# A second expert for 21 tokens: 128 places in a full array against 32 places in four column tiles

## The chip, the cores and the metric

The kernel runs on one core of one Trainium2 chip. The metric is device time in microseconds (us). A core has TensorE (PE in the profile; its weight loads are listed apart as PEld), VectorE (DVE), ScalarE (ACT), GpSimd (POOL) and SyncE (SP). DMAs are issued from the queues of SP, ACT and POOL and are carried out by 16 DMA engines that all of them share.

## The reference

Attention with one shared key and value head, and then a mixture of experts with two levels of routing:

```python
scores = scale * q @ k.T ; attn = softmax(scores) ; x = (attn @ v)  as [3072, 1024]
g = argmax(x @ w_group)                 # one of 4 groups
e = argmax(x @ w_expert[g])             # one of 4 experts of that group
h = relu(x[tokens of (g, e)] @ w1[g, e])
out[tokens of (g, e)] = group_weight * expert_weight * (h @ w2[g, e])
```

There are 8 batches of 384 tokens, 16 heads of 64, a model width of 1024, and 16 experts with a hidden width of 1024. Because attention averages over its batch, nearly all tokens of a batch choose the same expert. The routing is data dependent, and the inputs are fixed by a seed: evaluated on them, the reference sends all 384 tokens of each of the first seven batches to one expert, and of the last batch 363 tokens to one expert and 21 to a second one.

## The kernel before

**Tiling.** Tokens lie in batches of three blocks (`ST = 3`) of 128. The main loop over half units (line 794) does attention for one batch while the expert of the batch before it runs in the gaps of TensorE. `main_expert` (line 531) takes the most chosen expert of a batch and computes it for all 384 tokens: in its first part (line 479) a 128x128 block of `w1` is the loaded operand and 384 tokens stream by, in its second part (line 493) 128 hidden values by 128 tokens are loaded and 512 columns of `w2` stream by. Tokens that chose another expert get a factor of zero. The result `y` of 128 tokens is written by `store` as four DMAs on SP's queue (line 536), which together are three times four for a batch.

**The last batch.** After the loop (from line 827) there is no attention left for TensorE to share. The order is written out by hand: `advance(n)` runs the next pieces of the main expert, and pieces of the second expert's preparation stand between them. `few_ready` (line 540) builds constants on POOL. `few_turn` (584) turns the batch's activations into token order. `few_flags` and `few_places` (595, 609) find which tokens chose the second expert, number them 0, 1, 2, ... and build for each block of 128 tokens a 0/1 matrix `sel16`, whose column p marks the token on place p; there are 128 places. If more tokens chose it than there are places, `fits` is 0 and the pair is left to the loop at the end. `few_gather` (636) multiplies the token-ordered activations by `sel16`: 24 matmuls of 128 columns (line 643) give `xg`, the chosen tokens' activations with the model width on the partitions; three small matmuls (line 654) give each place its factor `gate` and its row number `at`, which for an empty place lies past the last row. `few_expert` (664) comes after the main expert's end and after `keep_xb(b)` (line 470: the batch's activations, 768 KB, to a scratch tensor in DRAM, on SP's queue). It is in the same form as the main expert, on 128 places: 64 matmuls (line 674) with blocks of `w1` loaded and 128 places streaming, relu by ACT and DVE (lines 680, 682), then 24 matmuls (line 689) with 128 hidden values by 128 places loaded and 512 or 256 columns of `w2` streaming, scaling by DVE and ACT (lines 695, 693), and one indirect DMA on POOL's queue (line 696) that writes each place's row of 4 KB to its row number and skips those past the end.

**Weights.** `load_w` (451) issues two DMAs of POOL's queue for each of `w1` and `w2`, each for half of the contracted blocks (`o` = 0 to 3 and 4 to 7), converting from float32 to bfloat16 on the way. For the second expert they are issued by `load_second(0)` and `load_second(1)` (lines 837, 844), long before `few_expert`. The matmuls that read blocks 4 to 7 wait for the second DMA only.

**The end.** Each engine then reads the number of remaining pairs (line 910) and enters a loop over them (line 911), which for these inputs has no passes.

Of the kernel before, what the change touches and what calls it, by code (L numbers as in the profile page):

```python
# [9 lines left out]
FP32 = mybir.dt.float32  # L10
# [9 lines left out]
def kernel(  # L20
# [23 lines left out]
    NP = B * GE  # L44
    NR = 4096
    assert NR > N
    assert NP == P
# [45 lines left out]
    def xbank():  # L93
        x = ps_x.tile([P, 512], FP32, tag="x", name="x")
        return x
# [354 lines left out]

    def load_w(e, n):
        w = wpool.tile([P, KO, F], BF16, tag=f"w{n + 1}", name="w")
        for o in range(0, KO, 4):
            nc.gpsimd.dma_start(  # L454
                out=w[:, o:o + 4, :], in_=(w1f, w2f)[n][ds(e, 1), :, o:o + 4, :].rearrange("o p c f -> (o p) c f")
            )
        return w
# [73 lines left out]
    def main_expert(b, on_act):  # L531
        w1, w2 = st.pop(("w", b))

        def store(j, y):
            for n in range(QN):
                nc.sync.dma_start(out=out_v[b, j, n], in_=y[32 * n:32 * (n + 1), :])

        yield from expert(st["xb", b], w1, w2, scaled(lambda: st["gsel", b][0], store), any_bank, on_act)

    def few_ready():  # L540
# [4 lines left out]
        for name, t, widths in (  # L545
            ("16", c16, (("eye", P), ("tri", P), ("sel", ST * P), ("f", 4), ("cum", 4), ("parts", 5 * ST))),
            ("32", c32, (
                ("cols", P), ("tri", P), ("sel", ST * P), ("prod", ST * GE), ("ohs", GE), ("rows", ST), ("rest", ST), ("row", 1), ("pos", 4),
                ("f", ST), ("fits", 1), ("gate", 1), ("low", 1), ("at", 1),
            )),  # L550
        ):
# [4 lines left out]
        nc.gpsimd.iota(  # L556
            fw["cols32"], pattern=[[1, P]], base=0, channel_multiplier=0, allow_small_or_imprecise_dtypes=True
        )
# [20 lines left out]
        fw["xt"] = [ppool.tile([P, Dm], BF16, tag="pr", name="xtok") for _ in range(ST)]  # L579
        fw["xg"] = ppool.tile([P, KO, P], BF16, tag="pr", name="xg")  # L580

# [27 lines left out]
    def few_places():  # L609
# [11 lines left out]
        for j in range(ST):  # L621
            nc.vector.tensor_scalar(
                out=fw["sel32"][:, ts(j, P)], in0=fw["cols32"], scalar1=pos[:, j:j + 1], scalar2=fw["f32"][:, j:j + 1],
                op0=ALU.is_equal, op1=ALU.mult,
            )
        nc.scalar.copy(out=fw["sel16"], in_=fw["sel32"])

# [8 lines left out]
    def few_gather():  # L636
        fw = st["few"]
        parts = fw["parts16"].rearrange("p (j t) -> p j t", t=5)
        for half in range(2):
            bank = xbank()  # L640
            for k in range(4):
                for j in range(ST):
                    nc.tensor.matmul(  # L643
                        out=bank[:, ts(k, P)], lhsT=fw["xt"][j][:, ts(4 * half + k, P)], rhs=fw["sel16"][:, ts(j, P)],
                        start=(j == 0), stop=(j == ST - 1),
                    )
            xg = fw["xg"][:, 4 * half:4 * half + 4, :].rearrange("p k t -> p (k t)")
            if half:
                nc.vector.tensor_copy(out=xg, in_=bank[:])
            else:  # L650
                nc.scalar.copy(out=xg, in_=bank[:])
        bank = xbank()
        for j in range(ST):
# [5 lines left out]
        nc.vector.tensor_scalar(  # L659
            out=fw["at32"].bitcast(I32), in0=fw["row32"], scalar1=fw["fits32"], scalar2=float(NR), op0=ALU.mult,  # L660
            op1=ALU.add,
        )

    def few_expert():

        fw = st["few"]
        w1, w2 = st.pop("w_second")
        xg, gate, at_ = fw["xg"], fw["gate32"], fw["at32"].bitcast(I32)
        h_t = pool.tile([P, FO, S], BF16, tag="hT", name="few_h", bufs=1)
        for k0, k1 in ((0, 4), (4, 6), (6, FO)):  # L670
            bank = xbank()[:, 0:(k1 - k0) * P]
            for k in range(k0, k1):
                for ko in range(KO):
                    nc.tensor.matmul(  # L674
                        out=bank[:, ts(k - k0, P)], lhsT=w1[:, ko, ts(k, P)], rhs=xg[:, ko, :],
                        start=(ko == 0), stop=(ko == KO - 1),
                    )
            h, hp = h_t[:, k0:k1, 0:P], bank.rearrange("p (k t) -> p k t", t=P)
            if k0 == 4:
                nc.vector.tensor_scalar(out=h, in0=hp, scalar1=0.0, scalar2=None, op0=ALU.max)  # L680
            else:
                nc.scalar.activation(out=h, in_=hp, func=ACTF.Relu)
        cols = ((0, 512), (512, 768), (768, Dm))
        ys = [xbank()[:, 0:z - a] for a, z in cols]
        y = pool.tile([P, Dm], FP32, tag="y", name="few_y", bufs=3)
        for part in range(2):
            for (a, z), yp in zip(cols, ys):
                for fo in range(4 * part, 4 * part + 4):
                    nc.tensor.matmul(  # L689
                        out=yp, lhsT=h_t[:, fo, 0:P], rhs=w2[:, fo, a:z], start=(fo == 0), stop=(fo == FO - 1)  # L690
                    )
                if part and a:
                    nc.scalar.activation(out=y[:, a:z], in_=yp, func=ACTF.Copy, scale=gate)
                elif part:
                    nc.vector.tensor_scalar(out=y[:, a:z], in0=yp, scalar1=gate, scalar2=None, op0=ALU.mult)
        nc.gpsimd.indirect_dma_start(
            out=out, out_offset=bass.IndirectOffsetOnAxis(ap=at_, axis=0), in_=y[:], in_offset=None,
            bounds_check=N - 1, oob_is_err=False,
        )
# [262 lines left out]
```

## Time and profile before

| | us |
|---|---|
| median of 3 runs | 509.74 |
| the 3 runs | 508.01, 509.74, 509.88 |
| the profiled execution's own time | 508.39 |
| span of the profiled execution (first to last instruction) | 507.0 |

| engine | busy us | share of the span |
|---|---|---|
| PE | 481.5 | 95% |
| DVE | 413.0 | 81% |
| ACT | 321.8 | 63% |
| POOL | 289.6 | 57% |

The chain of waits is the list of what ended last, followed back from the end: 90% of it is PE. A line of the timeline gives the start, the length, the engine, the source line, the operation, `out<-in`, shapes as partitions x elements, a count, and in brackets the idle time before it with what ended it; pieces of one group that lie close together are merged into one line. "128*32" behind a matmul's tensors is the part of the TensorE array that it uses, rows by columns. In a view by windows each row is a stretch of the span with the busy time of each engine, the granted TensorE clock, the busy share of the DMA engines (it can read a little over 1) and the GB/s moved. A DMA's time to landing runs from its issue to its completion. For groups of matmuls the busy time is the union of overlapping executions, so busy time over count is the pitch, and "mean ns of one" is the time from the start of one to its modelled end.

### The profile page before, as it was taken

The page shows a single profiled execution, that of the slowest core. Times are in us where ns is not written, and L with a number is a line of the kernel's source. Part 1 is how long each engine was busy: PE and PEld are TensorE (multiplying, and loading weights), DVE is VectorE, ACT ScalarE, POOL GpSimd, SP SyncE. Part 2 cuts the span into 40 slices and gives each one's busy share as a digit, 9 for nine tenths or more (in the row PEclk, how much of TensorE's full clock was granted, in tenths as well). Part 3 has the DMA queues.
Part 4 walks back from the last instruction along what each step waited for, and adds up shares of the span by engine and source line. Part 5 has one row for each costly group of instructions (what it writes and reads, how often), then busy time and mean ns, then how long its engine had stood idle before and what let it go on. Part 6 is the DMA issues. An engine that isn't in the chain of part 4 may idle for free.

```text
span 507.0 us, 20054 instructions
## 1 busy us (share of the span) xinstructions
PE 481.5 (95%) x8256; PEld 262.1 (52%) x8273; DVE 413.0 (81%) x737; ACT 321.8 (63%) x1002; POOL 289.6 (57%) x524
## 2 busy tenths in 40 slices
PE   7597789999999999999999999999999999999994
PEld 3143356555456455555465455555455455555653
DVE  3889979988899879988899879998799888890630
ACT  4776766677676766676676776676775775753421
POOL 1665955684576664584576654584476654584300
PEclk9999999999999999999999999999999999999998
DMA  7612997399947998389946998389956993089993
GB/s 106 145 26 45 174 239 193 76 160 233 255 86 129 220 237 218 75 157 232 261 84 123 217 243 223 75 143 230 245 116 111 210 241 110 1 155 241 231 243 121
DMA packets 64524, 84.04 MB, mean 166 GB/s; under 512 B 20379, under 2 KB 39963, under 8 KB 64432
## 3 DMA queue, kind: packets, MB, share of 16 engines
q0 software_dynamic: 19152, 37.84, 41.3%
q1 hardware_dynamic: 44320, 44.61, 35.2%
q8 instruction: 66, 1.08, 0.9%
q10 hardware_dynamic: 960, 0.30, 0.3%
q14 instruction: 26, 0.21, 0.1%
HBM read 101.52 MB, written 19.40 MB: 239 GB/s over the span
## 4 chain that ended last, share of the span: by engine, by line
PE 90%; DVE 5%; ACT 3%; issue 1%; POOL 0%; POOLq 0%; ACTq 0%; DVEq 0%
PE x L257 26%; PE s L206 25%; PE x L479 15%; PE x L493 13%; PE sb L493 4%; PE x L280 3%; ACT pr L220 3%; DVE nmx L217 2%; PE sb L479 2%; DVE ring L241 2%; PE x L674 1%; PE x L100 1%; PE x L689 1%; PE x L145 0%; PE x L643 0%
## 5 line engine op out<-in xcount | busy, mean ns | idle before, releaser
L235 POOL TENSOR_SCALAR pr<-pr,rinv 128x384 f32<-128x384 f32 x384 | 218.3, 588 | 146.0 <-DVE rinv L231 133.2
L220 ACT ACTIVATE pr<-s,nmx 128x384 f32<-128x384 f32 x384 | 218.0, 579 | 131.5 <-DVE nmx L217 120.0
L217 DVE TENSOR_REDUCE nmx<-s 128x2 f32<-128x768 f32 x192 | 174.3, 948 | 45.7 <-PE s L206 44.6
L241 DVE STREAM_TRANSPOSE ring<-pr 128x768 f32<-128x768 f32 x192 | 175.4, 952 | 0.1
L206 PE MATMUL s<-kt,qt 64*64 64x384 f32 x1536 | 148.9, 496 | 13.3 <-ACT pr L220 12.3
L257 PE MATMUL x<-ring,v_sb 32*64 32x256 f32 x4608 | 137.7, 378 | 0.2
L257 PEld LDWEIGHTS x<-ring,v_sb 32*64 32x64 f32 x4608 | 101.6, 131 | 43.0 <-issue 23.2
L206 PEld LDWEIGHTS s<-kt,qt 64*64 64x64 f32 x1536 | 48.5, 132 | 82.6 <-ACT pr L220 44.4
L220 ACT ACTIVATION_READ_ACCUMULATOR pr<-s,nmx 128x1 f32 x384 | 77.9, 203 | 0.0
L479 PE MATMUL x<-xb,w 128*128 128x384 bf16 x448 | 76.6, 326 | 0.0
L479 PEld LDWEIGHTS <-w 128*128 128x128 bf16 x512 | 47.7, 98 | 42.2 <-issue 12.6
L493 PE MATMUL x<-w,h_t 128*128 128x512 bf16 x276 | 64.7, 380 | 0.6
L493 PEld LDWEIGHTS <-h_t 128*128 128x128 bf16 x384 | 35.7, 98 | 52.0 <-issue 11.9
L454 POOL DMA_DIRECT2D w<-in_moe_w_dram x36 | 27.9, 784 | 10.8 <-issue 9.0
L271 ACT COPY xt<-x 128x256 f32<-128x256 f32 x96 | 28.9, 385 | 2.8 <-PE x L257 2.7
L485 ACT ACTIVATE h_t<-x 128x384 bf16<-128x384 f32 x56 | 25.4, 502 | 6.4 <-PE x L479 6.4
L272 POOL CAST xb<-xt 128x1024 bf16<-128x1024 f32 x24 | 24.9, 1036 | 3.6 <-ACT xt L271 3.6
L511 ACT ACTIVATE y<-x,gsel 128x512 f32<-128x512 f32 x36 | 24.8, 693 | 3.1 <-PE x L493 3.1
L195 DVE STREAM_TRANSPOSE qt<-q_sb 128x512 f32<-128x512 f32 x38 | 26.1, 687 | 0.0
L493 PE MATMUL sb<-w,h_t 128*128 128x512 bf16 x92 | 21.2, 379 | 0.2
L231 DVE RECIPROCAL rinv<-ssum 128x4 f32<-128x4 f32 x96 | 13.9, 144 | 3.3 <-ACT pr L220 3.3
L511 ACT ACTIVATE y<-sb,gsel 128x512 f32<-128x512 f32 x9 | 6.2, 688 | 16.1 <-PE sb L493 16.1
(132 smaller groups left out, 165.6 us busy)
## 6 DMA issues: line engine op xcount, KB each, us to landing
w<-in_moe_w_dram POOLq DMA_DIRECT2D x36, 1024.0 KB, 19.6
q_sb<-in_q_dram SPq DMA_DIRECT2D x76, 224.0 KB, 6.0
out_dram<-y SPq DMA_DIRECT2D x96, 128.0 KB, 6.3
xb_scratch<-xb SPq DMA_DIRECT2D x8, 768.0 KB, 4.3
v_sb<-in_v_dram SPq DMA_DIRECT2D x32, 96.0 KB, 4.0
kk<-in_k_dram SPq DMA_DIRECT2D x28, 92.0 KB, 4.1
q_sb<-in_q_dram SPq DMA_DIRECT2D x16, 128.0 KB, 3.3
q_sb<-in_q_dram SPq DMA_DIRECT2D x5, 64.0 KB, 3.1
```

Source lines behind the costliest of these rows:

```text
L195: nc.vector.transpose(out=qt[:].rearrange("p (x d) -> p x d", d=32), in_=q_sb[:, :, 0:32])
L206: nc.tensor.matmul(out=s[m * D:(m + 1) * D, h, 0:S], lhsT=qt[r, ts(2 * cc + m, D)], rhs=kt[r, :], start=True, stop=True, tile_position=(h ...
L217: nc.vector.tensor_reduce(out=nmx[:], in_=s[:, :, 0:S], axis=AX.X, op=ALU.max, negate=True)
L220: nc.scalar.activation(out=pr[:, h, :], in_=s[:, h, 0:S], func=ACTF.Exp, bias=nmx[:, h:h + 1], scale=1.0, accum_out=ssum[:, k, h:h + 1],)
L235: nc.gpsimd.tensor_scalar(out=pr, in0=pr, scalar1=rinv[:, k, h:h + 1], scalar2=1.0, op0=ALU.mult, op1=ALU.mult)
L241: nc.vector.transpose(out=ring[:, (u // 4) % 3, u % 4].rearrange("p h s -> p (h s)"), in_=st.pop(("pr", u))[:].rearrange("p h s -> p (h s)"),)
L257: nc.tensor.matmul(out=o[i][h * D:(h + 1) * D, 0:2 * P].rearrange("d (g c q) -> d g c q", g=2, c=4), lhsT=v_sb[r, n, :], rhs=ring[r, a:z + ...
L271: nc.scalar.copy(out=xt[:, :, ts(i, 32)], in_=o[:, 0:2 * P].rearrange("p (c q) -> p c q", c=KO))
L454: nc.gpsimd.dma_start(out=w[:, o:o + 4, :], in_=(w1f, w2f)[n][ds(e, 1), :, o:o + 4, :].rearrange("o p c f -> (o p) c f"))
L479: nc.tensor.matmul(out=hp[:, 0:S], lhsT=w1[:, ko, ts(fc, P)], rhs=xb[:, ko, :], start=(ko == 0), stop=(ko == KO - 1))
L493: nc.tensor.matmul(out=yp, lhsT=h_t[:, fo, ts(j, P)], rhs=w2[:, fo, ts(nh, 512)], start=(fo == 0), stop=(fo == FO - 1),)
L511: nc.scalar.activation(out=y[:, ts(nh, 512)], in_=yp, func=ACTF.Copy, scale=g)
```

## The change

The second expert's tokens get 32 places (`FEW`) in place of 128, repeated four times (`FQ`) over the 128 columns of `sel16`. The work is done as follows.

- `few_places`: `fits` compares with 32; a second flag `fits4` is four times `fits`; the three DVE operations write `sel16` directly, and ACT's copy from float32 is gone.
- `few_gather`: the 24 matmuls stream 32 columns in place of 128, into one bank, and one ACT copy of 256 columns takes the place of an ACT and a DVE copy of 512 each. The gate and row matmuls still give all 128 partitions a value, so each place has four partitions.
- `few_expert`: the roles of weights and tokens are exchanged. `few_rows` loads 128 model values by 32 places in one of four column tiles of the array, and streams 256 columns of `w1` by; the four tiles take the four quarters of the columns. 32 matmuls give 32 places x 1024 hidden values, folded into 128 partitions x 256. A DVE transpose in 32x32 blocks and a DVE maximum with zero bring the hidden values onto the partitions; the order of the hidden values that results is matched by loading `w2` for this expert through another view (`w2r`, in which partition p holds rows 8p to 8p+7). A second `few_rows` gives 32 places x 1024 outputs, again folded into 128 partitions x 256. One DVE operation scales them.
- The indirect DMA writes 128 quarter rows of 1 KB: partition 32c + p holds quarter c of place p, and its row number is four times the token's row plus c (`base`).
- `main_expert`'s `store`, for the last block of the last batch: two of the four DMAs are issued on ACT's queue, two on SP's.
- `few_ready`: four more memsets on POOL, a different pattern of the column numbers, and the buffers of the new shapes.

```diff
+    FEW = 32
+    FQ = P // FEW
...
+    w2r = moe_w2.rearrange("g e (fi fo) d -> (g e) fi fo d", fi=P)
+    out_q = out.rearrange("n (c d) -> (n c) d", c=FQ)
...
-        st.setdefault("w_second", []).append(load_w(st["e2"], n))
+        st.setdefault("w_second", []).append(load_w(st["e2"], n, (w1f, w2r)))
...
             for n in range(QN):
-                nc.sync.dma_start(out=out_v[b, j, n], in_=y[32 * n:32 * (n + 1), :])
+                queue = nc.scalar if b == B - 1 and j == ST - 1 and n % 2 else nc.sync
+                queue.dma_start(out=out_v[b, j, n], in_=y[32 * n:32 * (n + 1), :])
...
+        for c in range(FQ):
+            nc.gpsimd.memset(fw["base32"][ts(c, FEW), :], float(FQ * NR + c))
...
-        nc.vector.tensor_single_scalar(out=fw["fits32"], in_=pos[:, 3:4], scalar=float(P), op=ALU.is_le)
+        nc.vector.tensor_single_scalar(out=fw["fits32"], in_=pos[:, 3:4], scalar=float(FEW), op=ALU.is_le)
+        nc.vector.tensor_scalar(
+            out=fw["fits432"], in0=fw["fits32"], scalar1=float(FQ), scalar2=None, op0=ALU.mult
+        )
...
-                out=fw["sel32"][:, ts(j, P)], in0=fw["cols32"], scalar1=pos[:, j:j + 1], scalar2=fw["f32"][:, j:j + 1],
+                out=fw["sel16"][:, ts(j, P)], in0=fw["cols32"], scalar1=pos[:, j:j + 1], scalar2=fw["f32"][:, j:j + 1],
...
-        nc.scalar.copy(out=fw["sel16"], in_=fw["sel32"])
...
+        bank = xbank()
+        for k in range(KO):
+            for j in range(ST):
+                nc.tensor.matmul(
+                    out=bank[:, ts(k, FEW)], lhsT=fw["xt"][j][:, ts(k, P)], rhs=fw["sel16"][:, j * P:j * P + FEW],
+                    start=(j == 0), stop=(j == ST - 1),
+                )
+        nc.scalar.copy(out=fw["xg"], in_=bank[:, 0:KO * FEW])
...
+    def few_rows(lhs, w):
+
+        bank = xbank()
+        for o in range(KO):
+            for c in range(FQ):
+                nc.tensor.matmul(
+                    out=bank[ts(c, FEW), 0:256], lhsT=lhs[:, ts(o, FEW)], rhs=w[:, o, ts(c, 256)],
+                    start=(o == 0), stop=(o == KO - 1), tile_position=(0, c * FEW),
+                )
+        return bank[:, 0:256]
...
+        bank = few_rows(fw["xg"], w1)
+        nc.vector.transpose(
+            out=fw["h32"].rearrange("p (o t) -> p o t", t=FEW), in_=bank.rearrange("p (x o) -> p o x", o=FO)
+        )
+        nc.vector.tensor_scalar(out=fw["h16"], in0=fw["h32"], scalar1=0.0, scalar2=None, op0=ALU.max)
+        bank = few_rows(fw["h16"], w2)
+        nc.vector.tensor_scalar(out=fw["y32"], in0=bank, scalar1=fw["gate32"], scalar2=None, op0=ALU.mult)
         nc.gpsimd.indirect_dma_start(
-            out=out, out_offset=bass.IndirectOffsetOnAxis(ap=at_, axis=0), in_=y[:], in_offset=None,
-            bounds_check=N - 1, oob_is_err=False,
+            out=out_q, out_offset=bass.IndirectOffsetOnAxis(ap=fw["at32"].bitcast(I32), axis=0), in_=fw["y32"],
+            in_offset=None, bounds_check=FQ * N - 1, oob_is_err=False,
         )
```

More of the change, by code (lines that the diff above doesn't have):

```diff
@@ L547, in few_ready @@
             ("32", c32, (
-                ("cols", P), ("tri", P), ("sel", ST * P), ("prod", ST * GE), ("ohs", GE), ("rows", ST), ("rest", ST), ("row", 1), ("pos", 4),
-                ("f", ST), ("fits", 1), ("gate", 1), ("low", 1), ("at", 1),
+                ("cols", P), ("tri", P), ("prod", ST * GE), ("ohs", GE), ("rows", ST), ("rest", ST), ("row", 1), ("pos", 4),
+                ("f", ST), ("fits", 1), ("fits4", 1), ("gate", 1), ("low", 1), ("at", 1), ("base", 1),
             )),
@@ L579, in few_ready @@
         fw["xt"] = [ppool.tile([P, Dm], BF16, tag="pr", name="xtok") for _ in range(ST)]
-        fw["xg"] = ppool.tile([P, KO, P], BF16, tag="pr", name="xg")
+        xg = ppool.tile([P, 2 * KO * FEW], BF16, tag="pr", name="xg")
+        fw["xg"], fw["h16"] = xg[:, 0:KO * FEW], xg[:, KO * FEW:]
+        rest = pool.tile([P, 512], FP32, tag="qt", name="rest", bufs=3)
+        fw["h32"], fw["y32"] = rest[:, 0:KO * FEW], rest[:, KO * FEW:]
     def few_turn(j, half):
@@ L638, in few_gather @@
         parts = fw["parts16"].rearrange("p (j t) -> p j t", t=5)
[L639 to L651, printed above, removed]
+        bank = xbank()
[6 more added lines that the diff above has]
+        nc.scalar.copy(out=fw["xg"], in_=bank[:, 0:KO * FEW])
         bank = xbank()
@@ L667, in few_expert @@
         w1, w2 = st.pop("w_second")
[L668 to L695, printed above, removed]
+        bank = few_rows(fw["xg"], w1)
```

9 lines of the change are left out of this document (5 added, 4 removed).

## The prediction

> **What bounds the kernel now.** I read the page's chain of waits first (90% PE), then the same chain piece by piece over the last 30 us, because every edited line runs there. Columns: start us, us, what.
>
> ```profile
> 481.28 1.34 PE x L643 x24
> 482.62 0.06 PE x L654 x3
> ...
> 486.20 6.91 PE sb L493 x32
> 493.11 3.57 PE x L674 x64
> ...
> 499.30 0.04 DVEq L695
> 499.33 0.05 issue
> 499.38 0.76 DVE few_y L695
> ```
>
> Up to 493.11 TensorE runs without a hole, so what it saves in the gather moves everything behind it. The rest is a serial tail: expert, scaling, scatter. The timeline of that stretch:
>
> ```profile
> 492.94 3.74 PE L674 MATMUL x<-xg,w 128*128 128x128 bf16 x64
> 493.15 0.75 DVE L513 TENSOR_SCALAR y<-sb,gsel 128x512 f32<-128x512 f32 x1 [2.70 <-DMA out_dram<-y]
> 495.83 0.42 DVE L680 TENSOR_SCALAR few_h<-x 128x256 bf16<-128x256 f32 x1 [1.93 <-PE x L674]
> 496.00 0.36 SPq L470 DMA_DIRECT2D xb_scratch<-xb  x1
> 496.52 3.64 PE L689 MATMUL x<-w,few_h 128*128 128x512 bf16 x23
> 499.81 0.86 ACT L693 ACTIVATE few_y<-x,c 128x256 f32<-128x256 f32 x2 [2.70 <-PE x L689]
> 501.02 1.11 POOL L696 DMA_INDIRECT out_dram<-few_y,c  x1 [19.37 <-ACTq L911]
> ```
>
> From the expert's first matmul (492.94) to the scatter's start (501.02) pass 8.08 us. The scatter waits for ACT's scaling, which ends at 499.81 + 0.86 = 500.67, so a hand-over to POOL takes 0.35. The page gives the span as 507.0 us. Two DMA stories run beside this: the second half of `w2` and the copy of the activations on SP. The windows (busy us of PE, PEld, DVE, ACT, POOL; granted clock; DMA share; GB/s):
>
> ```profile
> 491.00:493.00 2.00, 2.00 (x11) 0.93 (x10) 0.00 (x0) 0.69 (x1) 0.00 (x0) 1.00 1.10 331
> 493.00:494.70 1.70, 1.70 (x33) 1.70 (x32) 0.75 (x1) 0.00 (x0) 0.00 (x0) 1.00 0.69 247
> 494.70:496.50 1.80, 1.80 (x36) 1.80 (x34) 0.42 (x1) 0.60 (x1) 0.00 (x0) 1.00 0.97 248
> 496.50:499.00 2.50, 2.45 (x19) 1.59 (x18) 0.00 (x0) 0.38 (x1) 0.00 (x0) 1.00 0.99 356
> ```
>
> The DMA engines are saturated until 493 and nearly so from 494.7 to 499. The clock is full wherever TensorE works.
>
> **The gather.** 24 matmuls at a pitch of 1.34 / 24 = 56 ns stream 32 columns instead of 128. What is left is the 128-column weight load. Nearest rows, short matmuls that each load 128 columns:
>
> ```profile
> 475.70 0.17 PE L612 MATMUL x<-c 128*128 128x4 bf16 x1
> 475.73 0.16 PE L613 MATMUL x<-c,ones 128*128 128x4 bf16 x1
> 475.75 0.32 PE L391 MATMUL x<-mask_all,ones 128*128 128x384 bf16 x1
> ```
>
> They start 20 to 30 ns apart. I take 27: 24 x 27 = 0.65, a gain of 0.69. Bounds: no gain if loads already pace the 56 ns, 0.86 at the 20 ns of the chain's line 654 (0.06 / 3). The ACT and DVE copies of `xg` lie beside the main expert before and after.
>
> **One pass of column tiles.** The trace has the shape: line 280 uses 128x32 tiles, four side by side, a new weight load for each matmul.
>
> ```profile
> L280 PE MATMUL x<-xt,wge 128*32 128x64 f32 x512 | 8.8, 220 | 0.0
> L280 PE MATMUL x<-xt,wge 128*32 128x32 f32 x512 | 6.1, 199 | 0.0
> L689 PE MATMUL x<-w,few_h 128*128 128x256 bf16 x16 | 2.1, 272 | 0.0
> ```
>
> Their pitches are 17 and 12 ns, so four tiles with four loads take 69 and 48 ns: the tiles run together, and four loads need at most 48 ns. In bfloat16, 256 columns take half of the chain's 6.91 / 32 = 216 ns for 512, so 108 ns, above the load limit. Eight groups: seven pitches and one full duration of 272 ns, 0.76 + 0.27 = 1.03 us. Bound above: the float32 slope (21 ns for 32 more columns) from 48 ns gives 195 ns a group, +0.6 a pass; below, nothing under 108 ns is in sight.
>
> The Trainium skill's page "TensorE: Matmul & The Clock Gate", Part 3 (packing small matmuls), says that weight loads overlap running matmuls only when their row group differs. Column tiles share their row group, so by that rule each tile would wait for the one before it, and the sum would be that of the third rival below. The two rows of line 280 disagree, with four matmuls and their loads in 48 ns; the same part reports a speedup of 2.38 for three column tiles, so the page does not hold to the strict reading either.
>
> The array changes form ahead of the first pass. The same change before line 280:
>
> ```profile
> 467.81 0.38 PE L493 MATMUL sb<-w,h_t 128*128 128x512 bf16 x1
> 468.12 0.24 PE L280 MATMUL x<-xt,wge 128*32 128x64 f32 x1
> ```
>
> 0.31 from start to start instead of 0.216, so 0.09 more.
>
> **Between the passes.** DVE rows for the transpose:
>
> ```profile
> L195 DVE STREAM_TRANSPOSE qt<-q_sb 128x512 f32<-128x512 f32 x38 | 26.1, 687 | 0.0
> L290 DVE STREAM_TRANSPOSE lg<-x 128x64 f32<-128x64 f32 x8 | 1.9, 241 | 12.9 <-PE x L280 12.9
> ```
>
> Between 241 ns at 64 and 687 at 512, 256 columns interpolate to 0.43; the strided read from PSUM is not shown in a transpose, bounds 0.24 and 0.69. The maximum: 0.42, the duration of line 680, which has its shape. The scaling of 256 columns: 0.42 by the same row, in place of 0.75 on DVE and 0.86 on ACT. Hand-overs from TensorE to DVE, as after L689 in the chain: about 0.08; I take it back to TensorE too, at most the 0.35 seen towards POOL. DVE's last scaling for the main expert ends at 493.90, and at 493.21 after the gather's gain, before the first pass ends (493.37).
>
> **The sum to the scatter's start.** 0.09 + 1.03 + 0.08 + 0.43 + 0.42 + 0.08 + 1.03 + 0.08 + 0.42 + 0.35 = 4.01, where 8.08 stood: 4.07 saved, with the gather 4.76. The scatter starts at 496.26.
>
> **The scatter.** The DMA view from 500.9 to 505, and its time to landing:
>
> ```profile
> DMA packets 146, 0.11 MB, mean 27 GB/s; under 512 B 123, under 2 KB 123, under 8 KB 144
> ...
> out_dram<-few_y,c POOLq DMA_INDIRECT x1, 2.8
> ```
>
> 144 - 123 = 21 packets lie between 2 and 8 KB, the rows of 4 KB: the second expert has 21 tokens, so 32 places suffice. Skipped rows cost a small packet too, so 128 indices should give about the same packet number, with 84 of 1 KB. The 1.11 on POOL stays. The 2.8 - 1.11 = 1.7 in flight could shrink towards nothing: 21 adjacent partitions before, four separate groups after. On the other side the scatter now falls into what is left of SP's copy. I cost it at nothing, bounds -1.2 and +0.6. What follows the landing is unchanged.
>
> **`w2` in the other view.** Issued at the same time; the row of its two DMAs:
>
> ```profile
> L454 POOL DMA_DIRECT2D w<-in_moe_w_dram x2: 760/775/790, 468.5 to 469.3; - x2
> ...
> DMA to landing us min/median/max: 19.7/22.5/25.4
> ```
>
> The second half lands at 469.3 + 25.4 = 494.7. Line 689 needs it after 4 x (216 + 2 x 108) ns, at 498.25: a cover of 3.6. After the change the second pass starts at 494.38 and needs it 4 x 108 ns later, at 494.81: a cover of 0.1. I keep the landing, because bytes and issue stay and the engines are saturated (1.10) while it moves; 16 KB of adjacent source bytes per partition could serve it earlier or later by some packets of the stores beside it, unknown, -1 to +3.
>
> **Stores on ACT, and SP behind them.** Rows of the stores and of the copy:
>
> ```profile
> L536 SPq DMA_DIRECT2D out_dram<-y x14: 314/420/554, 469.8 to 495.5; - x14
> DMA to landing us min/median/max: 3.7/4.3/6.4
> ```
>
> Two issues of 0.42 leave SP, so the copy is issued at 496.00 - 0.69 - 0.84 = 494.47 and lands, by line 470's own 3.7 to 6.4, between 498.2 and 500.9. The scatter lands at 496.26 + 2.8 = 499.06. At the median (498.8) the copy is hidden, with 0.3 of cover. Behind the two issues ACT has nothing that anyone waits for: its work for the second expert is gone.
>
> **Edits at nothing.** `fits4` (one small DVE operation) and the missing ACT copy lie ahead of a gather that starts at 481.28. The four memsets lie ahead of this:
>
> ```profile
> 465.62 1.04 POOL L272 CAST xb<-xt 128x1024 bf16<-128x1024 f32 x1 [3.64 <-ACT xt L271]
> 477.39 0.51 ACT L626 CAST c<-c 128x384 bf16<-128x384 f32 x1 [0.99 <-DVE c L622]
> ```
>
> POOL idles 3.64 before its next needed work, four memsets cost under 0.5; the matrix is ready at 477.90, 3.4 before its use. Without this cover each would cost its own length.
>
> **From the sum to the forecast.** 508.39 - 4.76 = 503.6 against the profiled execution, which is 1.35 under the median shown. The four times known (508.01, 508.39, 509.74, 509.88) have a mean of 509.0; from there the forecast is 504.2.
>
> **Rivals.**
> - *`w2` arrives late.* TensorE waits in the second pass, and a landing d later costs d - 0.1. For: the cover falls from 3.6 to 0.1 on saturated engines. Against: nothing adds bytes. With 2 us: 506.1. Chance 0.14.
> - *SP's copy sets the end.* It must land after 499.06; the end of its row, 500.9, costs 1.8: 506.0. For: the cover of 0.3. Against: the same bytes begin earlier, into the hole of 493 to 494.7 (share 0.69). Chance 0.09.
> - *The four tiles run one after another.* 32 x 108 ns = 3.46 a pass instead of 0.86, twice: +5.2, 509.4, no change. The rows of line 280 speak against it, though in float32. Chance 0.07. This is the rule of the Trainium skill's page "TensorE: Matmul & The Clock Gate", Part 3, taken to its end.
> - *The scatter becomes the bound, and the kernel slower.* If its 2.8 grows with the rows written, 21 to 84, it takes 11.2: +8.4, 512.6. It is even with the old median at 2.8 + 5.5 = 8.3 and slower by over 0.5% from 10.9. Against: packets hardly change and the bytes are the same. Chance 0.06.
> - *It does nothing*, because more than 32 tokens come and the pair falls to the loop: the 21 packets exclude it.
>
> **How the numbers follow.** The forecast as summed: 0.61; what is left, 0.03, is spread. Low end: 508.01 - 4.76 with 0.17 more in the gather and the scatter's 1.2, 501.9. High end: the forecast with `w2` 3.5 late, 507.6; tiles in turn, the slow scatter and little else lie outside. The likeliest case alone: 501.9 to 505.5. A measurement of this kernel tells about 0.5% (2.5 us) from no change: the forecast, the late `w2` and the copy are faster, 0.84; tiles in turn and part of the rest are the same, 0.09; the slow scatter and the remainder slower, 0.07.
>
> **What would show it.** Line 643's pieces at about 27 ns each; the two passes at about 1.0 us, 32 matmuls each, starting about 2 us apart with a transpose of 0.43 and a maximum of 0.42 between; the scatter 4 us behind the first pass's start; no wait for a DMA at the second pass; the copy landing before the scatter. Passes of 3.5 us, a hole in the second pass after 16 matmuls, or a landing far over 2.8 us would make the prediction wrong.

## The result

| | before | after |
|---|---|---|
| median of 7 runs, us | 509.74 | 507.38 |
| range of the runs, us | 508.01 to 509.94 | 505.55 to 507.81 |
| profiled execution: time, span, us | 508.39, 507.0 | 507.47, 506.0 |

The ratio of after to before is 0.9954, with a 95% interval of 0.9937 to 0.9971. The kernel became faster by 2.4 us (0.46%) where 5.5 were forecast: the interval lies clear of no change, but the gain is just within the 0.5% that the prediction counted as no change.

The two profiled executions differ by some 1.8 us before the gather. The rows are the windows of 12.5 to 25 us of the kernel before, of the kernel after, and of a second profiled execution of the same kernel after (busy us of PE, PEld, DVE, ACT, POOL; granted clock; DMA share; GB/s):

```profile
12.50:25.00 12.50, 6.79 (x61) 1.88 (x60) 10.97 (x16) 9.47 (x34) 7.99 (x15) 1.00 0.66 143
```

```profile
12.50:25.00 12.50, 8.63 (x60) 2.40 (x62) 10.20 (x15) 8.89 (x30) 8.18 (x15) 0.73 0.57 124
```

```profile
12.50:25.00 12.50, 7.12 (x68) 2.08 (x68) 11.01 (x17) 9.47 (x32) 7.56 (x15) 1.00 0.67 147
```

In the second row the granted clock was 0.73 in the mean (0.50 from 20 to 24 us); the third is the same code without that. About 1.0 us of the difference arises in that stretch: the fifth of DVE's row maxima (`nmx`) starts at 14.64, 14.93 and 14.09 in the three, the twelfth at 26.09, 27.42 and 25.54. The rest arises elsewhere, and its cause stays open. So steps are counted here from the first matmul of the second expert's first pass (before: line 674, at 492.94; after: line 677, at 494.15), and for the gather from its own first matmul. The timeline of the kernel after:

```profile
482.93 0.76 PE L655 MATMUL x<-c,xtok 128*128 128x32 bf16 x24
...
494.15 1.06 PE L677 MATMUL x<-w,xg 128*32 128x256 bf16 x32
...
495.26 0.45 DVE L688 STREAM_TRANSPOSE rest<-x 128x256 f32<-128x256 f32 x1 [0.25 <-PE x L677]
495.75 0.29 DVE L691 TENSOR_SCALAR xg<-rest 128x256 bf16<-128x256 f32 x1
...
496.09 1.06 PE L677 MATMUL x<-w,xg 128*32 128x256 bf16 x32 [0.88 <-DVE xg L691]
497.13 0.35 SPq L474 DMA_DIRECT2D xb_scratch<-xb  x1
497.21 0.48 DVE L693 TENSOR_SCALAR rest<-x,c 128x256 f32<-128x256 f32 x1 [1.17 <-PE x L677]
500.36 1.11 POOL L694 DMA_INDIRECT out_dram<-rest,c  x1 [16.84 <-issue]
```

The expert is ready at 497.21 + 0.48 = 497.69, 3.54 us after the first pass began, where the kernel before took 7.73. That part came out as summed. But the scatter starts at 500.36, 2.67 us later. The chain of waits says what it waited for:

```profile
483.09 0.59 PE x L655 x24
...
483.79 3.47 PE sb L497 x16
...
487.36 0.76 DVE y L517
...
488.53 6.91 DMA out_dram<-y
...
495.89 0.35 SPq L541
...
496.28 2.91 DMA out_dram<-y
...
499.51 0.62 issue
500.14 0.29 POOLq L908
500.43 1.04 POOL out_dram L694
```

TensorE, 90% of the chain before, is gone from the chain from 487.33 on. In its place stand two stores of the main expert: one of block 0, whose landing at 495.44 lets SP go on, and the last one, which lands at 499.19 and lets GpSimd go on. The scatter overwrites rows that these stores write, so it must come after them. The kernel before had the same wait. Its last store was issued at 495.48 and landed at 497.97, 5.02 us after the first pass's start; in the kernel after it is 5.04. These are the semaphore waits of POOL's queue ahead of line 696 (first and last start):

```profile
L696 POOLq EVENT_SEMAPHORE  x5: 43/43/1917, 497.7 to 498.3; - x5
```

The waits for stores were over by 498.3, and the last of the five, of 1.917 us, was one for DVE's scaling. So the landing lay hidden under an expert that was ready at 500.67.

### The profile page after: what moved, and what is told of

Its sections match the earlier page's. It is cut to its first block, busy times and chain, and to the rows that moved or that the text cites. A ratio compares the mean times of both kernels' runs of the same rounds, so it can differ in the third digit from the quotient of the medians.

```text
span 506.0 us, 20018 instructions
## 1 busy us (share of the span) xinstructions
PE 479.9 (95%) x8249; PEld 257.5 (51%) x8249; DVE 412.6 (82%) x738; ACT 319.6 (63%) x997; POOL 288.4 (57%) x528
## 4 chain that ended last, share of the span: by engine, by line
PE 88%; DVE 4%; ACT 2%; DMA 2%; issue 1%; POOL 0%; SPq 0%; POOLq 0%; ACTq 0%; DVEq 0%
PE x L261 26%; PE s L210 26%; PE x L483 15%; PE x L497 13%; PE sb L497 3%; PE x L284 3%; ACT pr L224 2%; DVE nmx L221 2%; PE sb L483 2%; DMA out_dram<-y 2%; DVE ring L245 1%; PE x L104 1%; PE x L149 0%; PE x L187 0%; PE x L598 0%
## 5 line engine op out<-in xcount | busy, mean ns | idle before, releaser
L210 PE MATMUL s<-kt,qt 64*64 64x384 f32 x1536 | 151.3, 504 | 12.0 <-ACT pr L224 9.9
L489 ACT ACTIVATE h_t<-x 128x384 bf16<-128x384 f32 x56 | 25.4, 502 | 6.6 <-PE x L483 6.6
```

Source lines behind the costliest of these rows:

```text
L210: nc.tensor.matmul(out=s[m * D:(m + 1) * D, h, 0:S], lhsT=qt[r, ts(2 * cc + m, D)], rhs=kt[r, :], start=True, stop=True, tile_position=(h ...
```

## The experiments

Steps in us from the first pass's start; "ready" is the end of the second expert's scaling. The ratio is to the kernel before on the same chip, with its 95% interval.

| kernel | ready | scatter starts | span ends | ratio |
|---|---|---|---|---|
| before | 7.73 | 8.08 | 14.06 | 1 |
| after | 3.54 | 6.21 | 11.85 | 0.9954 (0.9937 to 0.9971) |
| after, again | 3.53 | 6.12 | 12.06 | 0.9960 (0.9941 to 0.9978) |
| scatter elsewhere | 3.53 | 3.83 | 11.79 | 0.9953 (0.9934 to 0.9971) |
| before, scatter elsewhere | 7.72 | 8.04 | 14.08 | 0.9995 (0.9978 to 1.0011) |
| copy in the loop | 3.53 | 6.29 | 11.92 | 0.9929 (0.9906 to 0.9952) |
| both | 3.54 | 3.83 | 10.42 | 0.9904 (0.9877 to 0.9931) |
| before, copy in the loop | 7.72 | 8.08 | 14.17 | 0.9996 (0.9980 to 1.0013) |
| second pass twice | 4.41 | 6.11 | 11.87 | 0.9939 (0.9917 to 0.9962) |
| last stores all on SP | 3.53 | 6.80 | 12.45 | 0.9952 (0.9933 to 0.9971) |
| `w2` interleaved | 4.31 | 6.36 | 12.02 | 0.9938 (0.9914 to 0.9961) |
| half stores | 3.53 | 8.30 | 13.93 | 0.9997 (0.9981 to 1.0012) |
| half stores, copy in the loop | 3.53 | 8.27 | 13.88 | 0.9990 (0.9977 to 1.0004) |
| all odd stores on ACT | 3.53 | 6.10 | 11.76 | 0.9944 (0.9926 to 0.9962) |
| the same, copy in the loop | 3.53 | 5.76 | 11.36 | 0.9950 (0.9931 to 0.9968) |
| last odd stores on POOL | 3.53 | 7.66 | 13.37 | 0.9976 (0.9959 to 0.9992) |
| the same, copy in the loop | 3.54 | 5.79 | 11.59 | 0.9936 (0.9917 to 0.9956) |

In all of these traces the span ends 3.1 to 3.3 us after the scatter has landed, so the end moves with that landing. An interval is 0.8 to 1.4 us to each side, so differences of half a microsecond between the variants are read from the steps, each of one profiled execution, and not from the ratios.

**Is it the stores that hold the scatter?** The scatter writes to a tensor of its own, so the output lacks the second expert's 21 rows.

```diff
-    out_q = out.rearrange("n (c d) -> (n c) d", c=FQ)
+    elsewhere = nc.dram_tensor("elsewhere", [N, Dm], FP32).ap()
+    out_q = elsewhere.rearrange("n (c d) -> (n c) d", c=FQ)
```

> The changed kernel with the scatter aimed at another DRAM tensor; the 21 rows of the second expert in the output keep the main expert's zeros. Theory: in the changed kernel the scatter, which starts at 500.36 of 506.0, waits for the stores of the main expert's last rows, because they write the same tensor (last landing 499.19), and not for the second expert, whose result is there at 497.69. Without that wait the scatter starts 0.35 to 0.95 us after the scaling's end instead of 2.67, and 1.7 to 2.3 us are gained on the changed kernel (median 507.38, so 505.1 to 505.7, ratio to the kernel before about 0.991), unless SP's copy of the activations, whose last packets move at about 501, then sets the end, which would leave about 1. Rival (GpSimd's queue itself is late): the scatter still starts about 2.7 after the scaling and nothing is gained.

The timeline:

```profile
493.51 1.06 PE L678 MATMUL x<-w,xg 128*32 128x256 bf16 x32
...
496.32 0.35 SPq L475 DMA_DIRECT2D xb_scratch<-xb  x1
496.56 0.48 DVE L694 TENSOR_SCALAR rest<-x,c 128x256 f32<-128x256 f32 x1 [1.17 <-PE x L678]
497.34 1.11 POOL L695 DMA_INDIRECT elsewhere<-rest,c  x1 [14.46 <-DVE rest L694]
```

The wait is gone: the scatter starts 0.30 after the scaling, 2.38 earlier than in the changed kernel. So the stores held it. And yet the span ends where it did, 11.79 against 11.85. The DMA view of that stretch says where the 2.4 us went (KB each, time to landing):

```profile
xb_scratch<-xb SPq DMA_DIRECT2D x1, 768.0 KB, 4.3
...
elsewhere<-rest,c POOLq DMA_INDIRECT x1, 4.8
```

Issued beside SP's copy, the scatter needs 4.8 us to land and not 2.5.

**The same in the kernel before.** The line is that of `few_expert`'s scatter there.

```diff
-            out=out, out_offset=bass.IndirectOffsetOnAxis(ap=at_, axis=0), in_=y[:], in_offset=None,
+            out=elsewhere, out_offset=bass.IndirectOffsetOnAxis(ap=at_, axis=0), in_=y[:], in_offset=None,
```

> The kernel before with its scatter aimed at another DRAM tensor (the 21 rows stay zero). Theory: the same wait was there, ended at 498.3, and was hidden by an expert that ended at 500.67, so nothing changes: 509.7, within 0.3%. Rival (the scatter's handover is long in both kernels for a reason of its own): the same, but then the scatter elsewhere in the changed kernel gains nothing either.

Scatter at 8.04 and end at 14.08, as before: there the wait was covered. The scatter landed after 2.9 us (2.8), so another tensor is not slow by itself.

**The second cover.** The copy is moved into the loop, which has no passes.

```diff
-    keep_xb(b)
     few_expert()
...
         free.clear()
+        keep_xb(B - 1)
```

> The changed kernel with the copy of the last batch's activations moved into the loop over remaining pairs, which has no passes here, so that the copy does not run. Theory (two covers, one behind the other: the scatter waits for the stores, and behind that the copy's packets hold up what is in flight): the scatter still waits for the last store, which lands 0 to 0.6 earlier without the copy's packets beside it; gain on the changed kernel 0 to 0.7 us. Rival (the copy alone sets the end): a gain of 2 us or more.

Alone it moves nothing in the trace: scatter at 6.29, end at 11.92. The ratio is lower, but its interval overlaps that of the changed kernel. With the scatter elsewhere as well:

> The changed kernel with both removed: the scatter aimed at another DRAM tensor (the 21 rows stay zero) and the copy of the activations moved into the loop, where it does not run. Theory: now the scatter starts 0.3 after the scaling and is in flight for 2.5 us instead of 4.8, as in the changed kernel, so the span ends about 9.5 us after the first pass starts (11.85 in the changed kernel, 11.8 with the scatter elsewhere alone): 2.0 to 2.4 us less than the changed kernel, ratio to the kernel before about 0.991. That is the gain that the prediction had summed. Rival (a fixed floor at the end, whatever lands): the same time as the changed kernel.

```profile
494.18 1.06 PE L678 MATMUL x<-w,xg 128*32 128x256 bf16 x32
...
497.24 0.48 DVE L694 TENSOR_SCALAR rest<-x,c 128x256 f32<-128x256 f32 x1 [1.17 <-PE x L678]
498.01 1.11 POOL L695 DMA_INDIRECT elsewhere<-rest,c  x1 [14.46 <-DVE rest L694]
```

```profile
elsewhere<-rest,c POOLq DMA_INDIRECT x1, 3.5
```

The end comes at 10.42, 1.43 earlier, so the two covers lay one behind the other; the interval of the ratio, too, lies clear of the changed kernel's. It is less than expected: the scatter lands after 3.5 us and not 2.5. The main expert's last stores are not beside it: the last of their packets ended at 498.60, and the scatter's first one began at 499.69. Of the 16 steps by which the trace shows its completion semaphore rise, 15 came within 2.52 us, where the changed kernel has all 16 within 2.48, and one came at 3.45. A packet of 16 KB, of the queue that the profile calls instruction, lay beside the scatter's packets here (499.01 to 500.46), and in the changed kernel the last such packet ended 0.4 us before they began. Whether it is the cause is not shown.

> The kernel before with the copy of the activations moved into the loop, where it does not run. Theory: in the kernel before the expert sets the scatter's start and the copy has moved its packets by then, so nothing changes: ratio 1.000 within 0.002. Rival (the copy was on the path already): 1 us or more faster.

In the kernel before the copy cost nothing (8.08 and 14.17).

**Is the expert off the path?**

```diff
+        few_rows(fw["h16"], w2)
         bank = few_rows(fw["h16"], w2)
```

> The changed kernel with the second pass's 32 matmuls done twice, which makes the second expert about 0.9 us longer. Theory: the expert has 2.3 us of cover behind the stores' landing, so scatter and end stay where they are, 0 to 0.2 us. Rival (the expert is on the path, and the scatter is late for another reason): 0.9 us slower.

```profile
491.63 1.06 PE L677 MATMUL x<-w,xg 128*32 128x256 bf16 x32
...
493.57 1.93 PE L677 MATMUL x<-w,xg 128*32 128x256 bf16 x64 [0.88 <-DVE xg L691]
...
495.56 0.48 DVE L694 TENSOR_SCALAR rest<-x,c 128x256 f32<-128x256 f32 x1 [2.04 <-PE x L677]
497.74 1.11 POOL L695 DMA_INDIRECT out_dram<-rest,c  x1 [16.74 <-issue]
```

0.87 us more in the expert, and the end stays (11.87). A repetition of the changed kernel shows how far its steps can be trusted, some 0.2 us:

> The changed kernel as it is, beside the next three on one chip. Its steps counted from the first pass's start should be those of its first profile: scaling ends at 3.5, scatter starts at 6.2, span ends at 11.85 us; ratio to the kernel before 0.995.

**The stores' queues.** All four last stores on SP:

```diff
-                queue = nc.scalar if b == B - 1 and j == ST - 1 and n % 2 else nc.sync
-                queue.dma_start(out=out_v[b, j, n], in_=y[32 * n:32 * (n + 1), :])
+                nc.sync.dma_start(out=out_v[b, j, n], in_=y[32 * n:32 * (n + 1), :])
```

> The changed kernel with the four stores of the last block all on SP's queue again. Theory (the landing of the last store sets the scatter's start): SP's four issues take about 0.4 each in turn, so the last store is issued and lands about 0.8 later than now (about 500), the scatter starts as much later, and the kernel is 0.5 to 1 us slower than the changed kernel (about 508). Rival (the second expert or GpSimd sets the start): the same time as the changed kernel, 507.4.

From the chain of waits:

```profile
496.42 0.31 SPq L540
496.73 0.05 issue
496.79 3.20 DMA out_dram<-y
```

The last store is issued 0.3 later relative to the first pass than in the changed kernel (2.44 against 2.13 after it), lands 0.6 later, and the scatter follows by 0.6: the landing sets it. In the time this cannot be told from the changed kernel.

In this variant SP waits for no landing, and in the changed kernel it does. The trace names the completion semaphore that each DMA raises and those its queue waits for ahead of it. The stores of the changed kernel (start, queue, semaphore raised, semaphores waited for; 110 is raised by ACT's scaling and 101 by DVE's):

```
488.17 SP  sem 102 waits 102, 101, 110    block 0
488.53 SP  sem 103 waits 103
489.00 SP  sem 105 waits 105
489.46 SP  sem 106 waits 106
491.62 SP  sem 107 waits 107, 101, 110    block 1
491.98 SP  sem 109 waits 109
494.62 SP  sem 102 waits 102
495.10 ACT sem 108 waits 101, 110         block 2
495.46 SP  sem 103 waits 103              block 1
495.48 ACT sem 100 waits -                block 2
495.89 SP  sem 105 waits 105, 101, 110
496.28 SP  sem 106 waits 106
```

Eight semaphores go round. ACT's two stores take 108 and 100, so block 1's last two stores get 102 and 103 again and SP, which issues its DMAs in the order of the program, stands until block 0's first two have landed (494.60 and 495.44). Block 2's rows are ready at 495.01, and SP issues its first store of them at 495.89. Both variants that change this:

```diff
-                queue = nc.scalar if b == B - 1 and j == ST - 1 and n % 2 else nc.sync
+                queue = nc.scalar if b == B - 1 and n % 2 else nc.sync
```

> The changed kernel with the odd stores of all three blocks of the last batch on ACT's queue, not only those of the last block. Theory (SP issued the last block's stores late because it first waited for a landing of block 0's stores, 495.44 where the rows were ready at 495.01): with fewer stores on SP that wait is gone, the last block's stores are issued right after the scaling, the last landing and the scatter come 0.3 to 0.6 us earlier than in the changed kernel (scatter 5.6 to 5.9 after the first pass's start, in place of 6.1 to 6.2). The span gains 0 to 0.6, because the copy's packets then stand closer before the scatter's. Rival (SP's wait has another cause): a wait on a landing stays and the scatter starts at 6.1 to 6.2.

> The same, with the copy moved into the loop, where it does not run. Theory: both covers are as short as the stores allow: scatter at 5.5 to 5.9 after the first pass's start, span end at 11.1 to 11.5 (11.85 in the changed kernel), 0.4 to 0.7 us faster than the changed kernel. Rival: as above, 11.85.

A wait of SP on a landing stays, 0.7 and 0.3 us: here the twelve stores alternate, and block 2's second pair again meets block 0's. The scatter starts at 6.10 and 5.76, the span ends at 11.76 and 11.36. With GpSimd's queue for the two odd stores:

```diff
+                queue = nc.gpsimd if b == B - 1 and j == ST - 1 and n % 2 else nc.sync
```

> The changed kernel with the two odd stores of the last block on GpSimd's queue in place of ACT's. Theory (the DMAs of SP and ACT take their completion semaphores in turn out of eight, and ACT's two stores take two that would have gone to block 1's last stores, which so reuse semaphores of block 0's stores and hold SP until those land): GpSimd's DMAs use other semaphores, so SP no longer waits for a landing, block 1's four stores go out together as in the kernel before, and the last block's two SP stores are issued at 0.95 and 1.3 us after the first pass's start (1.74 and 2.13 now). The scatter starts at 5.4 to 5.8 (6.1 to 6.2 now) if GpSimd's two stores land as soon; the span gains 0 to 0.5. Rival (SP's wait has another cause): a wait of SP on a landing stays.

> The same, with the copy moved into the loop, where it does not run. Theory: scatter at 5.4 to 5.8 after the first pass's start, span end at 10.9 to 11.4 (11.85 in the changed kernel, 11.9 with the copy in the loop alone): 0.4 to 0.9 us faster than the changed kernel. Rival: GpSimd's own issue and landing are slower, and the end stays at 11.8 or comes later.

Block 1's four stores now go out in a row (490.90 to 493.12 with the copy kept), and SP's waits for a store's landing ahead of another store shrink to 0.2. The last block's first store goes out 0.94 after the first pass's start, where it was 1.74. So the shared rotation was what held SP. It does not help with the copy kept, because GpSimd's last store then lands only after 4.6 us (the chain of waits):

```profile
495.51 4.61 DMA out_dram<-y
...
500.24 0.62 issue
500.86 0.29 POOLq L908
501.15 1.05 POOL out_dram L694
```

Without the copy it is 2.75, and the scatter starts at 5.79.

**Half stores.** The last block's first 512 columns are stored as soon as they are scaled, the last 512 are scaled by DVE and ACT (256 each) and stored on SP and ACT; the copy is kept, or moved into the loop.

```diff
+            if halves and j == ST - 1:
+                if nh == 0:
+                    nc.scalar.activation(out=y[:, 0:512], in_=yp, func=ACTF.Copy, scale=g)
+                else:
+                    nc.vector.tensor_scalar(
+                        out=y[:, 512:768], in0=yp[:, 0:256], scalar1=g, scalar2=None, op0=ALU.mult
+                    )
+                    nc.scalar.activation(out=y[:, 768:Dm], in_=yp[:, 256:512], func=ACTF.Copy, scale=g)
+                halves(j, nh, y)
+                return
...
+        def store_half(j, nh, y):
+            for n in range(QN):
+                queue = nc.scalar if nh and n % 2 else nc.sync
+                queue.dma_start(
+                    out=out_v[b, j, n][:, ts(nh, 512)], in_=y[32 * n:32 * (n + 1), ts(nh, 512)]
+                )
```

> The changed kernel with the last block stored in two halves of its columns: the first 512 columns as soon as they are scaled (four DMAs on SP), the last 512 scaled by DVE and ACT side by side (256 each) and stored by two DMAs on SP and two on ACT. The copy stays. Theory (the landing of the last store sets the scatter's start): the last half is scaled 0.3 earlier and half as large, its landing comes 0.5 to 1.5 us earlier, and scatter and end move forward by as much less what the copy's packets then hold up: 0.3 to 1.0 us faster than the changed kernel. Rival (four more DMAs make SP wait for earlier landings): no gain, or a loss of up to 0.5.

> The same half stores with the copy moved into the loop, where it does not run. Theory: both covers shrink, the scatter starts 4.5 to 5.2 us after the first pass's start (6.2 in the changed kernel) and the span ends 10.3 to 11.0 after it (11.85): 0.9 to 1.5 us faster than the changed kernel, ratio to the kernel before about 0.992. Rival as for the half stores alone: no gain beyond that of the copy (0 to 0.3).

The outcome is the rival's, at more than its price. From the timeline with the copy kept:

```profile
492.57 0.48 DVE L518 TENSOR_SCALAR y<-sb,gsel 128x256 f32<-128x256 f32 x1 [2.70 <-PE sb L497]
493.09 0.47 ACT L521 ACTIVATE y<-sb,gsel 128x256 f32<-128x256 f32 x1 [1.51 <-DVE y L518]
...
494.21 4.26 SPq L555 DMA_DIRECT2D out_dram<-y  x6
```

ACT scales after DVE and not beside it. SP reaches its first half store at 494.21, after it has waited for landings of block 0 ahead of block 1's last two stores, as in the changed kernel. Then its six half stores stretch over 4.26 us. By the semaphores none of these six waits for a landing, so this is not the rival's mechanism; single issues take up to 1.37, and why is not shown. The scatter starts at 8.30, and the kernel is back at the time of the one before.

**The packets of `w2`.** In eight DMAs of one block each:

```diff
+        step = 1 if views[n] is w2r else 4
+        for o in range(0, KO, step):
             nc.gpsimd.dma_start(
-                out=w[:, o:o + 4, :], in_=views[n][ds(e, 1), :, o:o + 4, :].rearrange("o p c f -> (o p) c f")
+                out=w[:, o:o + step, :], in_=views[n][ds(e, 1), :, o:o + step, :].rearrange("o p c f -> (o p) c f")
```

> The changed kernel with this expert's second weight matrix loaded by eight DMAs of one block in place of two of four blocks, so that a packet is again 2 KB as before the change and not 8 KB. Theory (large packets take the engines from the stores beside them: the first store of block 0 landed after 6.4 to 6.9 us, before 5.0 to 5.8, and SP waited for such a landing from 492.8 to 495.4 before it issued the last block's stores): the landings go back to about 5.5 us, SP's wait on a DMA disappears, the last stores are issued about 0.4 earlier, and 0.3 to 0.5 us are gained on the changed kernel. Rival (packet size does not matter, the stores are slow for another reason): landings stay at 6.4 to 6.9 and the time at 507.4. Where the eight issues cost GpSimd more than that, the second pass waits for the weights.

The ratio was 1.0199 (1.0172 to 1.0227), for another reason than the one tested. GpSimd's queue, with more weight DMAs in flight, waited for landings of earlier ones, and everything it had to do for the second expert stood behind:

```profile
POOL w L459 <- DMA w<-in_moe_w_dram: 11.1, 3, 5.8
```

```profile
PE x L624 <- DVE c L616: 9.2, 1, 9.2
```

(Waiting engine and line, what it waited for, us in total, times, longest.) TensorE stood 9.2 us for the second expert's places. Block 0's stores were then issued after the last of these weights had landed (491.42), and landed after 1.9 to 2.2, which says nothing of packets. The test that does tell keeps two DMAs, of even and of odd blocks:

```diff
+            s = slice(o // 4, KO, 2) if views[n] is w2r else slice(o, o + 4)
             nc.gpsimd.dma_start(
-                out=w[:, o:o + 4, :], in_=views[n][ds(e, 1), :, o:o + 4, :].rearrange("o p c f -> (o p) c f")
+                out=w[:, s, :], in_=views[n][ds(e, 1), :, s, :].rearrange("o p c f -> (o p) c f")
```

> The changed kernel with the two DMAs of this expert's second weight matrix taking the even and the odd blocks, so that neither side is contiguous over blocks and packets are 2 KB again with two issues. Question: do 8 KB packets delay the stores beside them? Theory: the landings of block 0's stores go from 6.4 to 6.9 us back to 5.0 to 5.8; the last stores are not beside these packets, so the kernel's time stays within 0.3 us of the changed kernel's. Rival (packet size does nothing): landings stay at 6.4 to 6.9, and the same time.

Time to landing of block 0's four stores, first the changed kernel, then the interleaved one:

```profile
DMA to landing us min/median/max: 6.4/6.5/6.9
```

```profile
DMA to landing us min/median/max: 5.0/5.6/6.1
```

5.0 to 6.1 is what the kernel before shows for its own. So the large packets did delay the stores beside them, by about 0.9 us at the median, and thereby SP: with the small ones it issues the last block's first store 0.08 after the rows are ready, in place of 0.88. The scatter gains nothing by it (6.36), because ACT's second store then takes 4.0 us to land. Here, too, both DMAs of `w2` are needed from the second pass's fifth matmul on, and `w2` was late by 0.6, inside the cover of the stores' landing:

```profile
494.61 0.95 PE L678 MATMUL x<-w,xg 128*32 128x256 bf16 x28 [0.60 <-DMA w<-in_moe_w_dram]
```

No version that computes everything beats the changed kernel by more than the intervals tell; by its steps the best of them is the one with all odd stores on ACT and the copy in the loop, 0.5 us ahead of it.

## Why the prediction was wrong

The direction was right, and the size was off by more than a factor of two: 5.5 us forecast, 2.4 measured.

- **What held.** The gather was to gain 0.69 and gained 0.75 (0.59 for its piece of the chain instead of 1.34). With the change of the array's form behind it, put at 0.09, the sum had 0.60; from the gather's first matmul to the first pass 11.22 us went by instead of 11.83, so 0.61. A pass was put at 1.03 and took 1.06, and the four tiles do run together in bfloat16: 32 matmuls at N = 256 in 1.06 us, with 32 weight loads of one row group, 0.78 us busy, inside the same stretch. The rule of the Trainium skill's page "TensorE: Matmul & The Clock Gate", Part 3, that weight loads overlap running matmuls only across row groups, did not show here. The transpose took 0.45 (0.43), the strided read from PSUM costing nothing that can be seen; the maximum 0.29 (0.42), the scaling 0.48 (0.42). From the first pass to the scatter the sum said 3.92; with the stores' wait taken away it was 3.83. `w2` was on time: its second half landed at 470.9 + 24.4 = 495.3, and the second pass began at 496.09. The scatter's own cost stayed at 1.11 on POOL, with 2.5 in all where 2.8 had stood. What follows the landing stayed, too, at 3.14.
- **The step that failed** is "The sum to the scatter's start". It took the hand-over from DVE as all that the scatter waits for, and missed the landing of the main expert's stores, a wait that the kernel before had too. Its trace has that landing at 497.97, which less the gather's gain is 497.28. The step should have set the expert's 496.26 against that, and taken the later of the two. In the changed kernel the landing came 5.04 after the first pass's start and the scatter 1.17 behind it, so 6.21 stands where the sum had 3.92 (4.01 without the 0.09 ahead of the pass). From the first pass's start on, 8.08 - 3.92 = 4.16 were to be saved, and 14.06 - 11.85 = 2.21 were measured. Of the 1.95 that are missing, the wait took 2.38; some 0.4 came back through an expert 0.09 shorter than summed and a landing of 2.5 instead of 2.8.
- **The scatter in flight** was bounded at -1.2 to +0.6. With the stores' wait gone, it was 4.8 beside the copy where 2.8 had stood, +2.0; without the copy 3.5, so the copy holds 1.4 of it. The rival "SP's copy sets the end" was this in kind: it is hidden under the stores' landing, and comes out once that is gone. The number of packets did not stay about the same, either: the trace has 48 for the scatter in place of 144, 20 of them of 4 KB and 4 of about 1 KB, where 84 of 1 KB were expected.
- **Stores on ACT.** "Two issues of 0.42 leave SP" left out that SP and ACT share the rotation of completion semaphores. The copy was to be issued 2.1 us after the first pass's start and was at 2.98; SP issued the last block's stores 0.88 after its rows were ready.
- **Tiles in turn, the slow scatter and the late `w2`** did not occur. The cover of `w2` was put at 0.1 and was 1.3: its second half, needed 0.43 into the second pass at 496.52, landed at 495.26, because its DMA took 24.4 us instead of 25.4. With packets of 2 KB, in the interleaved version, that DMA took 25.9 and landed 2.79 after the first pass's start. The order of blocks of the changed kernel needs it at 2.37, so, as an estimate from these rows, the large packets kept `w2` in time.
- **The base.** The forecast counted from 509.0 and the median before is 509.74. From there the summed 4.76 would give 504.98, and 507.38 was measured: 2.4 are missing, of which 2.0 are those of the failed step. The other 0.4 is not explained. It lies within what single executions differ by ahead of the gather, which starts at 481.11 before, and at 482.93 and 480.01 in two executions of the kernel after.

## What to carry to other kernels

Before summing what a shorter chain saves, list every semaphore that its last instruction waits for, with the time at which each was satisfied in the old trace; the latest of those that stay is the floor. A write that overwrites part of an earlier write inherits that write's landing, and a DMA issued beside a large copy can land later by it. Moving a DMA to another queue can hold up the first one, where the queues share completion semaphores in rotation.

## What the runs showed of the hardware that was not expected

- Weight packets of 8 KB instead of 2 KB lengthened the landing of 128 KB stores beside them from 5.0 to 6.1 us to 6.4 to 6.9, and shortened that of the weights' second DMA from 25.4 to 24.4.
- A scatter of 84 KB took 2.5 us to land with no copy and no store beside it, 3.5 when it was issued earlier without the copy, for a reason not shown, and 4.8 when it was issued beside a copy of 768 KB.
- From the end of the last semaphore wait of POOL's queue to the scatter's start 0.85 us passed, in the kernel after (499.51 to 500.36) and in the kernel before (500.17 to 501.02, where that wait was for DVE). Where the scatter went elsewhere, and the queue had no such waits ahead of it, it started 0.30 after DVE's scaling.
- Weight loads of 128 columns keep up with matmuls of 32 columns at 25 ns each (0.59 us for 24, the chain's piece of line 655).
- Two executions of the kernel after differ in the clock granted in the first 25 us (0.73 or 1.00 over a window of 12.5 us), and by 2.7 us in span; about 1.0 of that arises in the stretch of low clock.
